# A gelu's square moved from ScalarE to GpSimd, in a kernel that interleaves attention and a dense layer

## The chip, the cores and the metric

The kernel runs on one core of a Trainium2 chip. The metric is device time in microseconds (us). The engines are named as the profile names them: PE (TensorE matmul), PEld (TensorE weight load, which overlaps PE), DVE (VectorE), ACT (ScalarE), POOL (GpSimd) and SP (SyncE, which issues DMAs).

## The reference

An input `x` of 2048 tokens by 512 features goes through two branches, and a gate of each token mixes them.

```python
g = sigmoid((x * gate_w).sum(-1, keepdims=True))
# a: attention, 32 heads of 16, each query sees the 256 latest keys
q, k, v = split_heads(x @ wqkv)
scores = where(mask, q @ k.T * 16 ** -0.5, -1e9)
a = (softmax(scores) @ v) @ wo
# b: dense layer with a tanh gelu, 512 -> 1792 -> 512
b = gelu(x @ w1 + b1, approximate=True) @ w2 + b2
out = g * a + (1 - g) * b
```

The gelu of x1 is 0.5 x1 (1 + tanh(0.79788 (x1 + 0.044715 x1^3))). The kernel forms it as (1 + tanh(GS * x1 * (x1^2 + GC))) * x1, with GC = 1/0.044715 and GS = 0.79788 * 0.044715, and leaves the factor 0.5 to a later step.

## The kernel before, in words

**Precision.** Every dense product is made of three matmuls: each operand is split into a rounded high part and the low remainder, and high*high, high*low and low*high are summed in PSUM (`mm3`, L101 to L103). So every weight and every hidden tile has a split: one copy to the high part, one subtract for the low part. For weights that is ACT (L156) and, for those of the dense layer, POOL (L160).

**Dense work.** The program `dense` first makes q, k, v in four token tiles of 512 (`qkv`), then runs the dense layer in eight turns of `mlp` (two halves of the hidden features, four token tiles each), and last the output projection (`final`). A turn makes seven products `u` [128 features x 512 tokens], each of 12 matmuls into one of two PSUM banks (`d`). Each `u` is given to `gelu`, which makes a tile `h` (high and low part). Then the turn makes four products `y` [128 tokens x 512], each of which takes the seven `h` in order with three matmuls each (21 matmuls into one bank). The weights of the second half are loaded and split in later parts of the run, some of them during the last turn of the first half.

**Attention.** It goes in 128 units (8 groups of four heads by 16 blocks of 128 tokens). In each unit TensorE makes four products `sm` (L389), whose row maxima DVE takes (L394, tile `jm` and `M`), and, six units later, four products `st` (L433), whose exp ACT takes into `pt` (L445). POOL zeroes the corners of `pt` outside the window (L437, L440), and TensorE multiplies `pt` with v (`pv`, L465). Every second unit the row maxima are negated and split on DVE (`nm`, L405 and L406), turned by a matmul (`mp`, L413) and written by ACT as extra rows of `qs` (L418). `sm` has three PSUM banks, `st` two, `pv` one.

**What sets the order.** PE, ACT, DVE and POOL each carry out their instructions in the order in which the program issues them. A small planner sets it: a modelled time `now` goes forward with each matmul issued, and `after(ns, fn)` puts a step into a list that is issued when `now` has reached its due time. `fill` pulls dense matmuls between the attention's matmuls, some 2345 ns of modelled dense work for each unit. `need(key)` issues steps early where a later one depends on them. So the due times are no delays on the chip: they set where a step stands in its engine's queue.

**The gelu.** Each gelu is a chain of seven steps over one 128x512 f32 tile, by their due times after the first:

- x1 = u + b1, on ACT, out of PSUM (L556)
- f1, sq = (u + b1)^2, on ACT, out of PSUM again (L559)
- f2, sq = (sq + GC) * x1, on DVE (L562)
- f3, tanh of sq, on ACT (L565)
- f4, x1 = (sq + 1) * x1, on DVE (L568)
- f5, the high part of h, a copy on DVE (L571)
- f6, the low part of h, a subtract on POOL (L574)

`x1` and `sq` are SBUF tiles with two buffers each. `GELU` (L749) holds the due times of f1 to f6.

Of the kernel before, what the change touches and what calls it, by code (L numbers as in the profile page):

```python
# [12 lines left out]
AF = mybir.ActivationFunctionType  # L13
# [19 lines left out]
def gated_mix(ctx: ExitStack, tc: tile.TileContext, x, wqkv, wo, w1, b1, w2, b2, gate_w, out):  # L33
    nc = tc.nc
# [10 lines left out]
    def f32(ap):  # L45
        return ap.bitcast(F32)
# [23 lines left out]
    b1c = cp.tile([128, NF], F32, name="b1c")  # L70
# [37 lines left out]
    def after(ns, fn, *args):  # L108
        now[1] += 1
        heapq.heappush(todo, (now[0] + ns, now[1], fn, args))  # L110
# [441 lines left out]
    def gelu(p, f, h):  # L552

        x1 = sb.tile([128, T], F32, tag="x1", bufs=2, name=f"x1{h.name}")
        sq = sb.tile([128, T], F32, tag="sq", bufs=2, name=f"sq{h.name}")
        nc.scalar.activation(x1, p, AF.Identity, bias=b1c[:, f:f + 1])  # L556

        def f1():
            nc.scalar.activation(sq, p, AF.Square, bias=b1c[:, f:f + 1])  # L559

        def f2():
            nc.vector.scalar_tensor_tensor(sq, sq, GC, x1, op0=ALU.add, op1=ALU.mult)  # L562

        def f3():
            nc.scalar.activation(sq, sq, AF.Tanh, scale=GS)  # L565

        def f4():
            nc.vector.scalar_tensor_tensor(x1, sq, 1.0, x1, op0=ALU.add, op1=ALU.mult)  # L568

        def f5():  # L570
            nc.vector.tensor_copy(h[:, 0], x1)  # L571

        def f6():
            nc.gpsimd.tensor_sub(h[:, 1], x1, f32(h[:, 0]))  # L574
            done.add(h.name)
        for ns, fn in zip(GELU, (f1, f2, f3, f4, f5, f6)):
            after(ns, fn)
# [168 lines left out]
LEAD = 6  # L746
START = 117e3
NORM = 6000
GELU = (700, 1500, 2300, 3300, 4200, 5000)  # L749
XAT = 3  # L750
ORDER = 'mspf'
XOR = 1
# [26 lines left out]
```

## Time and profile before

| | us |
|---|---|
| median of 3 runs | 812.53 (812.45 to 814.32) |
| the profiled execution | 813.36 |
| its span in the profile | 811.4 |
| PE busy | 788.5 (97%) |
| PEld busy | 616.6 (76%) |
| DVE busy | 513.7 (63%) |
| ACT busy | 483.4 (60%) |
| POOL busy | 338.7 (42%) |

A busy time is the sum of an engine's instructions in the profile. The ends of matmuls are modelled, so a busy PE can hold waits that the weight loads (PEld) show better. The granted TensorE clock is at its full value in every part of the span. The first gelu starts at 153.8 us from the span's start, the last at 727.8.

### The profile page before, as it was taken

Reading aid. Unit: us, or ns where it says so; the run is one execution under the profiler, and the core shown is the slowest. Engines: PE = TensorE matmul, PEld = TensorE weight load, DVE = VectorE, ACT = ScalarE, POOL = GpSimd, SP = SyncE. Lnnn points to the kernel's source line nnn. Section 1 sums busy time; section 2 is a strip of 40 time slices with the busy share of each in tenths; the row PEclk is TensorE's granted clock in tenths of the full one; section 3 lists DMA queues with packets and bytes.
Section 4 is the critical chain, followed back from the end, with each engine's and each line's share of the span. In section 5 each row is a group of like instructions: output and inputs, shape, how many; then the busy total and the mean of one; then the engine's idle time right before and its main releaser. Section 6 shows DMA issues by size and latency. Waiting matters only on the chain.

```text
span 811.4 us, 14841 instructions
## 1 busy us (share of the span) xinstructions
PE 788.5 (97%) x4694; PEld 616.6 (76%) x4694; DVE 513.7 (63%) x1517; ACT 483.4 (60%) x993; POOL 338.7 (42%) x611
## 2 busy tenths in 40 slices
PE   8999999999999999999999999999999999999998
PEld 6788888867877777688767867877777778777767
DVE  5433332887478758856885688568757865784353
ACT  4434423587568557755875677567656764876631
POOL 3200002396336425542784386336524552574100
PEclk9999999999999999999999999999999999999999
DMA  8985856536542734443234555542664363335873
GB/s 260 387 308 195 304 174 211 195 89 215 164 137 66 227 116 119 122 156 104 86 101 132 171 156 173 152 143 86 192 179 129 99 202 113 97 118 186 249 260 117
DMA packets 94925, 135.72 MB, mean 167 GB/s; under 512 B 32256, under 2 KB 43776, under 8 KB 94848
## 3 DMA queue, kind: packets, MB, share of 16 engines
q1 hardware_dynamic: 94848, 134.79, 52.3%
q8 instruction: 37, 0.61, 0.3%
q14 instruction: 40, 0.33, 0.1%
HBM read 79.70 MB, written 55.05 MB: 166 GB/s over the span
## 4 chain that ended last, share of the span: by engine, by line
PE 78%; DVE 8%; ACT 7%; DMA 2%; issue 2%; SPq 1%; POOL 1%; POOLq 0%; DVEq 0%; ACTq 0%
PE st L433 9%; PE pv L465 9%; PE sm L389 8%; PE y L101 6%; PE y L103 6%; PE y L102 6%; PE u L101 4%; PE u L102 4%; PE u L103 4%; PE qk L101 3%; PE qk L103 3%; PE qk L102 3%; DVE jm L394 2%; ACT pt L445 2%; PE v L103 2%
## 5 line engine op out<-in xcount | busy, mean ns | idle before, releaser
L394 DVE CUSTOM_DVE_ANT_0 jm<-sm,mask 128x384 bf16<-128x384 f32 (+2 forms) x512 | 270.6, 528 | 150.1 <-PE sm L389 128.7
L445 ACT ACTIVATE pt<-st 128x384 f32<-128x384 f32 (+2 forms) x512 | 231.0, 471 | 120.6 <-PE st L433 102.9
L437 POOL TENSOR_SCALAR_AFFINE_SELECT pt<-pt 128x256 f32<-128x256 f32 x256 | 122.3, 478 | 248.8 <-ACT pt L445 248.2
L433 PE MATMUL st<-qs,ks 128*128 128x384 f32 (+2 forms) x512 | 172.1, 338 | 8.1 <-ACT pt L445 7.1
L389 PE MATMUL sm<-ks,qs 96*128 96x384 f32 (+2 forms) x512 | 169.6, 332 | 1.8 <-DVE M L394 0.8
L433 PEld LDWEIGHTS st<-qs,ks 128*128 128x128 f32 x512 | 97.0, 190 | 37.1 <-ACT pt L445 19.4
L389 PEld LDWEIGHTS sm<-ks,qs 96*128 96x128 f32 x512 | 96.2, 188 | 26.0 <-DVE M L394 5.2
L440 POOL TENSOR_SCALAR_AFFINE_SELECT pt<-pt 128x256 f32<-128x256 f32 x224 | 101.9, 455 | 0.0
L465 PE MATMUL pv<-pt,vbuf 128*32 128x384 f32 (+2 forms) x1408 | 91.6, 389 | 0.1
L101 PE MATMUL y<-w,h 128*128 128x512 f32 x224 | 89.4, 399 | 0.0
L103 PE MATMUL y<-w,h 128*128 128x512 f32 x224 | 87.7, 391 | 1.3 <-POOL h L574 1.3
L102 PE MATMUL y<-w,h 128*128 128x512 f32 x224 | 87.7, 391 | 0.0
L574 POOL TENSOR_TENSOR h<-x1h,h 128x512 fp32r<-128x512 f32 x56 | 72.5, 1294 | 35.6 <-DVE h L571 35.2
L101 PE MATMUL u<-mx,w 128*128 128x512 f32 x196 | 79.3, 404 | 0.0
L102 PE MATMUL u<-mx,w 128*128 128x512 f32 x196 | 76.7, 391 | 0.0
L103 PE MATMUL u<-mx,w 128*128 128x512 f32 x196 | 76.6, 391 | 0.0
L418 ACT ACTIVATE qs<-mp,odd 16x256 fp32r<-16x256 f32 x128 | 53.0, 460 | 38.9 <-PE mp L413 37.9
L465 PEld LDWEIGHTS pv<-pt,vbuf 128*32 128x32 f32 x1408 | 38.5, 109 | 37.2 <-issue 24.2
L562 DVE SCALAR_TENSOR_TENSOR sqh<-sqh,x1h 128x512 f32<-128x512 f32 x56 | 51.6, 921 | 13.2 <-ACT sqh L559 13.2
L565 ACT ACTIVATE sqh<-sqh 128x512 f32<-128x512 f32 x56 | 35.5, 634 | 36.8 <-DVE sqh L562 36.2
L160 POOL TENSOR_TENSOR w<-raw_w,w 128x512 fp32r<-128x512 f32 x28 | 38.4, 1370 | 40.3 <-ACT w L156 40.2
L256 DVE TENSOR_TENSOR qke<-qk,qke 128x512 fp32r<-128x512 f32 x32 | 22.1, 691 | 51.3 <-ACT qke L253 49.6
(122 smaller groups left out, 1247.7 us busy)
## 6 DMA issues: line engine op xcount, KB each, us to landing
mx<-XT SPq DMA_DIRECT2D x24, 512.0 KB
SQ<-qke SPq DMA_DIRECT2D x16, 512.0 KB
SK<-qke SPq DMA_DIRECT2D x16, 512.0 KB
qs<-SQ SPq DMA_DIRECT2D x64, 128.0 KB
ND<-nd SPq DMA_DIRECT2D x32, 256.0 KB
ks<-SK SPq DMA_DIRECT2D x60, 128.0 KB
raw_w<-in_B_w_dram SPq DMA_DIRECT2D x28, 256.0 KB
SV<-vx SPq DMA_DIRECT2D x16, 272.0 KB
```

The costliest lines, as they stand in the source:

```text
L101: nc.tensor.matmul(p, lh, rh, start=first, stop=False)
L102: nc.tensor.matmul(p, lh, rl, start=False, stop=False)
L103: nc.tensor.matmul(p, ll, rh, start=False, stop=last)
L389: nc.tensor.matmul(p[:, :w], qs[0:96, pr, b * 128:(b + 1) * 128], ks[0:96, pr, s, k0:k0 + w], start=True, stop=True)
L394: nc.vector.tensor_tensor_reduce(junk[:, :w], p[:, :w], mask[:, 384 - w:384], 1.0, -3e38, ALU.add, ALU.max, M[:, b % RB, i:i + 1])
L418: nc.scalar.activation(qs[96:112, :, cols], p[96:112].unsqueeze(1).broadcast_to([16, 2, 128]), AF.Copy, scale=odd[96:112, b:b + 1])
L433: nc.tensor.matmul(p[:, :w], ks[:, pr, s, kb * 128:(kb + 1) * 128], qs[:, pr, kb * 128:kb * 128 + w], start=True, stop=True)
L437: nc.gpsimd.affine_select(out=pt[:, :, 0:128], in_=pt[:, :, 0:128], pattern=[[0, 2], [1, 128]], compare_op=ALU.is_ge, fill=0.0, base=0, ch ...
L440: nc.gpsimd.affine_select(out=pt[:, :, 256:384], in_=pt[:, :, 256:384], pattern=[[0, 2], [-1, 128]], compare_op=ALU.is_ge, fill=0.0, base= ...
L445: nc.scalar.activation(pt[:, s, :w], p[:, :w], AF.Exp, scale=SCALE)
L465: nc.tensor.matmul(pv[32 * i:32 * i + 32, q - c * T:e - c * T], vt[:, 68 * (kb % NB) + 17 * i:68 * (kb % NB) + 17 * i + 32], pts[g_, kb, i ...
L574: nc.gpsimd.tensor_sub(h[:, 1], x1, f32(h[:, 0]))
```

## The change

The square is formed on POOL, as x1 times x1 out of SBUF, and no longer on ACT out of PSUM. The due times of f2 to f6 move 700 ns later; that of f1 stays.

```diff
         nc.scalar.activation(x1, p, AF.Identity, bias=b1c[:, f:f + 1])
 
         def f1():
-            nc.scalar.activation(sq, p, AF.Square, bias=b1c[:, f:f + 1])
+            nc.gpsimd.tensor_mul(sq, x1, x1)
 
         def f2():
             nc.vector.scalar_tensor_tensor(sq, sq, GC, x1, op0=ALU.add, op1=ALU.mult)
...
-GELU = (700, 1500, 2300, 3300, 4200, 5000)
+GELU = (700, 2200, 3000, 4000, 4900, 5700)
```

## The prediction

> **What bounds the kernel now.** I read the page first, for the engines and the chain that ended last; then stretches of time, to find where TensorE loses anything; then what TensorE's weight loads waited for; then the groups by line; last, single instructions in order of time.
>
> ```profile
> PE 788.5 (97%) x4694; PEld 616.6 (76%) x4694; DVE 513.7 (63%) x1517; ACT 483.4 (60%) x993; POOL 338.7 (42%) x611
> ...
> PE 78%; DVE 8%; ACT 7%; DMA 2%; issue 2%; SPq 1%; POOL 1%; POOLq 0%; DVEq 0%; ACTq 0%
> ```
>
> TensorE is the bound by share, but a fifth of the chain runs over other engines. To see where, I cut the attention part into stretches of eight attention units (32 score matmuls each). Eight stretches hold the `u` products and so the gelus (first table: four of them and the sum of all eight); seven hold only `y` products between the same attention work (second table: the last and the sum). The columns are us, then the busy time of PE, PEld, DVE, ACT and POOL with counts.
>
> ```profile
> 157.10:197.30 40.20, 37.94 (x217) 28.71 (x216) 35.35 (x93) 31.38 (x65) 34.11 (x44) 1.00 0.43 132
> ...
> 383.70:423.30 39.60, 38.19 (x233) 29.04 (x233) 33.59 (x95) 33.26 (x69) 29.78 (x43) 1.00 0.36 104
> 460.80:502.40 41.60, 39.11 (x233) 28.86 (x232) 35.69 (x97) 33.41 (x70) 30.97 (x43) 1.00 0.49 145
> ...
> sum 316.60, PE 304.47 PEld 230.24 DVE 265.75 ACT 249.06 POOL 210.36; mean PE 38.06 PEld 28.78 DVE 33.22 ACT 31.13 POOL 26.30
> ```
>
> ```profile
> 652.70:689.10 36.40, 36.40 (x249) 28.97 (x248) 21.62 (x81) 19.50 (x45) 13.49 (x31) 1.00 0.50 158
> sum 254.40, PE 253.05 PEld 201.08 DVE 148.87 ACT 135.14 POOL 91.51; mean PE 36.15 PEld 28.73 DVE 21.27 ACT 19.31 POOL 13.07
> ```
>
> A `y` stretch takes 254.40/7 = 36.34 us, with TensorE never idle in the row shown. A `u` stretch takes 316.60/8 = 39.58. So the gelu stretches lose 316.60 - 8 x 36.34 = **25.9 us** in all, and nothing is lost elsewhere that this change touches. In them DVE is 84% busy, ACT 79%, POOL 66%: no engine is full, so the loss is in-order queues making TensorE wait. Who did it, over the whole of these stretches:
>
> ```profile
> PEld st L433 <- ACT pt L445: 19.2, 38, 1.4
> PEld mp L413 <- issue: 11.1, 28, 0.6
> PEld mp L413 <- DVE M L394: 6.6, 16, 0.6
> PEld mp L413 <- DVE nm L406: 5.4, 8, 1.5
> PEld sm L389 <- DVE M L394: 5.2, 13, 0.9
> PEld sm L389 <- ACT qs L418: 2.7, 5, 0.9
> PEld mp L413 <- DVE sqh L562: 2.1, 4, 0.6
> PEld y L103 <- POOL h L574: 1.8, 1, 1.8
> PEld pv L465 <- POOL pt L440: 1.3, 6, 0.2
> ```
>
> "Issue" names nobody and I leave it out. ACT: 19.2 + 2.7 = 21.9. DVE: 6.6 + 5.4 + 5.2 + 2.1 = 19.3. POOL: 1.8 + 1.3 = 3.1. These are idle times of the weight loads, which overlap with matmuls; together 44.3 against 25.9 us really lost, a factor 0.58. So ACT costs 12.8 us of time, DVE 11.2, POOL 1.8. Work that each engine does in the `u` stretches beyond the `y` ones: ACT 249.06 - 8 x 19.31 = 94.6, DVE 265.75 - 8 x 21.27 = 95.6, POOL 210.36 - 8 x 13.07 = 105.8. That gives an average price of one us of added work: **ACT 0.135, DVE 0.117, POOL 0.017** us. It is an estimate of mine; near a full queue the next us costs more than the average one. I use it as a scale.
>
> **The change, part by part.**
>
> **ACT loses the second pass (a gain).**
>
> ```profile
> L559 ACT ACTIVATE sqh<-u,b1c 128x512 f32<-128x512 f32 x56 | 38.5, 687 | 0.0
> ```
>
> 56 x 687 ns = 38.5 us. At the average price that is 38.5 x 0.135 = 5.2 us. Does it sit in the way of the exps that TensorE waits for? In 17 of the 30 longest waits of a score matmul for an exp this pass ran just ahead of the exps (in the last of them with one weight split between). First and last of the 17:
>
> ```profile
> 183.48 0.68 ACT L559 ACTIVATE sqh<-u,b1c 128x512 f32<-128x512 f32 x1
> ...
> 184.59 0.19 PEld L433 LDWEIGHTS st<-qs,ks 128*128 128x128 f32 x1 [0.75 <-ACT pt L445]
> ...
> 717.98 0.19 PEld L433 LDWEIGHTS st<-qs,ks 128*128 128x128 f32 x1 [0.71 <-ACT pt L445]
> ```
>
> 17 x 0.687 x 0.58 = 6.8 us. In the others the tanh held ACT while it waited for DVE, and that stays. Ends: 0 (the next wait takes over) and -12.8 (all of ACT's share); I take **-6**, between 5.2 and 6.8. The PSUM bank of `u` is read once and free 0.69 us sooner; no row shows TensorE waiting for it, so 0.
>
> **POOL gains 56 products.** Nothing shows this exact form; the nearest row is the subtract with two f32 operands of the same size.
>
> ```profile
> L574 POOL TENSOR_TENSOR h<-x1h,h 128x512 fp32r<-128x512 f32 x56 | 72.5, 1294 | 35.6 <-DVE h L571 35.2 <-DVE nm L405 0.4
> L160 POOL TENSOR_TENSOR w<-raw_w,w 128x512 fp32r<-128x512 f32 x28 | 38.4, 1370 | 40.3 <-ACT w L156 40.2
> ```
>
> 56 x 1.294 = 72.5 us, nearly all in the `u` stretches: 210.4 + 72.5 = 282.8 of 316.6, or 89%, fuller than DVE is now. In the first stretch, where POOL also splits weights, 34.11 + 6 x 1.294 = 41.9 us of work stand against 40.2 us of time. POOL takes its queue in order: behind a late square stand the selects of `pt` (then pv on TensorE), the weight splits and the previous gelu's subtract. Ahead of it may stand a subtract or a split, 1.3 us. And the first DVE step, L562, now waits for POOL: with POOL free, 0.687 + 1.294 = 1.98 us after x1 starts, where two ACT passes took 2 x 0.687 = 1.37; its slot moves by 0.7, so that alone costs nothing, but any POOL delay is passed on. Behind L562 on DVE stand the row maxima that free TensorE's `sm` banks, the `nm` that the next `mp` needs, and the tanh on ACT with the exps behind it. Price: low, POOL's average now, 72.5 x 0.017 = 1.2 us; high, the price that ACT and DVE show at 79 and 84% busy, 72.5 x 0.135 = 9.8. At 89% it is nearer to the high end: **+6**.
>
> **Two engines in each other's way.**
>
> ```profile
> L562 DVE SCALAR_TENSOR_TENSOR sqh<-sqh,x1h 128x512 f32<-128x512 f32 x56 | 51.6, 921 | 13.2 <-ACT sqh L559 13.2
> L568 DVE SCALAR_TENSOR_TENSOR x1h<-sqh,x1h 128x512 f32<-128x512 f32 x56 | 42.8, 764 | 7.5 <-ACT sqh L565 7.5
> ...
> L406 DVE SCALAR_TENSOR_TENSOR nm<-M,nm 128x8 fp32r<-128x8 f32 x64 | 17.7, 277 | 2.2
> ```
>
> ```profile
> L562 DVE SCALAR_TENSOR_TENSOR sqh<-sqh,x1h x56: 677/775/1775, 155.1 to 730.6; 128x512 f32<-128x512 f32 x56
> ...
> L568 DVE SCALAR_TENSOR_TENSOR x1h<-sqh,x1h x56: 682/689/1739, 156.9 to 732.4; 128x512 f32<-128x512 f32 x56
> ...
> L406 DVE SCALAR_TENSOR_TENSOR nm<-M,nm x64: 167/171/1279, 142.4 to 738.2; 128x8 fp32r<-128x8 f32 x64
> ```
>
> ```profile
> 401.02 1.28 POOL L160 TENSOR_TENSOR w<-raw_w,w 128x512 fp32r<-128x512 f32 x1
> ...
> 401.50 1.35 DVE L562 SCALAR_TENSOR_TENSOR sqh<-sqh,x1h 128x512 f32<-128x512 f32 x1
> ```
>
> The second fence has minimum, median and maximum of one instruction. L562 takes 677 ns alone, and 1.35 us here, beside a POOL subtract. Stretching now: 56 x 0.244 = 13.7, 56 x 0.082 = 4.6, 64 x 0.110 = 7.0 us: 25.3 us, over 84 POOL subtracts 0.30 us each. A square cannot meet its own gelu's DVE steps, only its neighbour's, so between 0 and 56 x 0.30 = 16.9 us of DVE; half, 8.4, at 0.117 to twice that is 1.0 to 2.0: **+1.5**; ends 0 and 16.9 x 0.234 = 4.0.
>
> The Trainium skill, page "SBUF — State Buffer", section "SBUF: two separate sides", says that VectorE and GpSimd share one pair of ports as an exclusive lock, and that the one who comes second waits until the other's instruction is over. The row agrees: 402.30 plus 0.68 would end at 402.98, and L562 ended at 402.85.
>
> **The five later steps move by 700 ns.** Each of the eight turns makes seven `h` tiles, and `y` takes them in order; the seventh's subtract was late once and barely in time another time:
>
> ```profile
> 426.49 0.50 PE L103 MATMUL y<-w,h 128*128 128x512 f32 x1 [1.35 <-POOL h L574]
> ```
>
> ```profile
> 733.59 1.29 POOL L574 TENSOR_TENSOR h<-x1h,h 128x512 fp32r<-128x512 f32 x1 [2.07 <-DVE h L571]
> ```
>
> ```profile
> 735.34 0.39 PE L103 MATMUL y<-w,h 128*128 128x512 f32 x1
> ```
>
> The one turn already waited, so all of the 0.7 is lost; the last turn has 735.34 - (733.59 + 1.29) = 0.46 of slack and loses 0.24: 0.9 us at least. With one more POOL product ahead (1.29): 1.99 + 1.53 = 3.5. I take **+2**. The `x1` buffers, held 0.7 longer, I cost at nothing: two of them cover the next gelu's 5.65 us (316.6/56) twice.
>
> **Sum:** -6 + 6 + 1.5 + 2 = **+3.5 us**. The profiled execution took 813.36 us (811.4 of span, 1.96 around it), so 816.9 of its own; it lies 0.83 above the median of the three runs, 812.53, on which I put the forecast: **816.0**.
>
> **Rivals.**
>
> *The relief of ACT wins.* POOL stands idle before the selects for long (it waits for exps), so the square could start as x1 ends and L562 find it done. Then -6.8 + 1.2 (POOL at its average) + 0.5 + 0.9 = -4.2: 808.3. It decides where L562's idle before it stays at its 13.2 us or under; against it stands POOL's 66% in these very stretches. Chance 0.30.
>
> *Both sides cancel*: the exps come sooner, DVE's steps as much later, 812.5. Chance 0.18.
>
> *POOL becomes the bound where weights are split* (the three stretches shown). With squares these hold 41.9, 29.78 + 9.06 = 38.8 and 30.97 + 9.06 = 40.0 us of work; if POOL is idle for a tenth besides (DVE at its fullest, 35.35 of 40.20, for an eighth), they need 46.5, 43.1 and 44.5 in place of 40.2, 39.6 and 41.6: +12.7, and with the other terms (-6 + 1.5 + 2) +10.2: 822.7. For it speaks that the work already fits into none of the first stretch's 40.2 us, against it that a `y` stretch follows with POOL a third busy. Chance 0.12.
>
> *Every DVE step that meets a square waits it out.* L568, the copy and about one `nm` step come in each 5.65 us; 3.1 x 1.294/5.65 = 0.71 meetings of 0.65 us, 26 us of DVE, at twice the price 6.1 us in place of 1.5: 820.6. Chance 0.07. That is the skill's rule on the shared ports taken in full.
>
> **How the numbers follow.** About 0.3% (2.4 us) is what can be told from no change. The forecast, slower by some us, gets 0.33 and by itself covers 813.5 to 821. Slower: 0.33 + 0.12 + 0.07 = 0.52; same 0.18; faster 0.30. Range: below, ACT's gain toward -9 with the rest near its low ends (0.9 + 0.5 + 2) gives -5.6; above, no gain with 9.8 + 4.0 would be +14: 807 to 826.
>
> **What would show it.** L559's group gone from ACT, a POOL group of 56 at about 1.3 us in its place. ACT's waits of `st` from 19.2 to about 10. L562's idle now ended by POOL, above 20 us; L562's mean at or above 921 ns. `y` waiting for `h` in more than one turn. `u` stretches at 320 us in sum, `y` stretches unchanged. Wrong if L562 hardly waits for POOL, or if TensorE's waits for `mp` and `sm` do not grow.

## The result, and the profile after

The changed kernel took **853.9 us** (median of 5 runs, 852.57 to 856.44) against 812.53 for the kernel before: ratio 1.0507, 95% interval 1.0484 to 1.0530. It is slower by 41 us, where I had forecast 3.5 and a range up to 826. One execution among the experiments (of the square due sooner) took 1272.79 us at a granted clock of 0.557, where all others had 0.98 or more; it is in no median here.

The page of the changed kernel, its first lines and the engines on the chain that ended last:

```profile
span 850.9 us, 14785 instructions
...
PE 799.7 (94%) x4694; PEld 619.7 (73%) x4694; DVE 535.3 (63%) x1517; ACT 453.1 (53%) x937; POOL 401.7 (47%) x667
...
PE 64%; DVE 13%; POOL 8%; ACT 6%; issue 5%; DMA 2%; SPq 0%; POOLq 0%; DVEq 0%
```

ACT lost 30 us, POOL gained 63. (A busy time of the page counts the overlap of two records once, so ACT's fell by less than the 38.5 us of the pass.) No engine but TensorE is over two thirds busy, and yet the chain now runs over DVE and POOL for a fifth of the span (9% before). The stretches of eight attention units again, cut at the same units: first the sum of the eight with `u` products, then of the seven with `y` products alone.

```profile
sum 352.50, PE 313.10 PEld 233.57 DVE 282.83 ACT 220.72 POOL 264.38; mean PE 39.14 PEld 29.20 DVE 35.35 ACT 27.59 POOL 33.05
```

```profile
sum 257.20, PE 254.46 PEld 200.59 DVE 153.07 ACT 134.78 POOL 96.59; mean PE 36.35 PEld 28.66 DVE 21.87 ACT 19.25 POOL 13.80
```

The `u` stretches grew from 316.6 to 352.5 us, +35.9 of the 39.5 us by which the span grew; the `y` stretches grew by 2.8, mostly at their starts, where `y` waits for the last `h`. What TensorE's weight loads waited for from the first to the last of these stretches:

```profile
PEld st L433 <- ACT pt L445: 41.7, 43, 3.1
PEld pv L465 <- issue: 22.6, 108, 0.3
PEld mp L413 <- DVE nm L406: 11.7, 12, 2.3
PEld mp L413 <- issue: 10.2, 25, 0.6
PEld sm L389 <- DVE M L394: 8.7, 14, 1.3
PEld mp L413 <- DVE M L394: 7.0, 16, 0.6
PEld sm L389 <- ACT qs L418: 4.0, 5, 1.7
PEld y L103 <- POOL h L574: 2.8, 3, 1.6
```

The wait for the exps is no shorter for an ACT with less to do: it doubled, 19.2 to 41.7. Why, the page's groups say (busy and mean of one, then the idle time before it and who ended it):

```profile
L565 ACT ACTIVATE sqh<-sqh 128x512 f32<-128x512 f32 x56 | 35.3, 631 | 101.9 <-DVE sqh L562 101.9
...
L562 DVE SCALAR_TENSOR_TENSOR sqh<-sqh,x1h 128x512 f32<-128x512 f32 x56 | 61.6, 1101 | 31.4 <-POOL sqh L559 31.1
...
L559 POOL TENSOR_TENSOR sqh<-x1h 128x512 f32<-128x512 f32 x56 | 60.4, 1078 | 8.7 <-ACT x1h L556 8.7
```

The tanh (L565) holds ACT idle for 101.9 us while it waits for L562; in the kernel before it was 36.2:

```profile
L565 ACT ACTIVATE sqh<-sqh 128x512 f32<-128x512 f32 x56 | 35.5, 634 | 36.8 <-DVE sqh L562 36.2
```

L562 waits 31 us for POOL's square and then takes 1101 ns in the mean. Minimum, median and maximum of the square and of L562:

```profile
L559 POOL TENSOR_TENSOR sqh<-x1h x56: 1032/1042/1474, 153.5 to 766.7; 128x512 f32<-128x512 f32 x56
...
L562 DVE SCALAR_TENSOR_TENSOR sqh<-sqh,x1h x56: 681/872/1767, 154.9 to 768.2; 128x512 f32<-128x512 f32 x56
```

Half of the L562 take over 872 ns, where the shortest take 681. Does POOL hold them? As L562 started, a POOL instruction was already running, with 100 ns or more to go, in 49 of the 56 cases (30 in the kernel before). For 35 of them DVE had stood idle; in 33 of these 35 POOL's next instruction had begun 66 to 88 ns before L562 (21 selects, seven weight splits, five subtracts), and these 33 took 1195 ns in the mean, the other two 693. One case in order of time:

```profile
510.86 1.05 POOL L559 TENSOR_TENSOR sqh<-x1h 128x512 f32<-128x512 f32 x1
...
511.86 1.27 POOL L160 TENSOR_TENSOR w<-raw_w,w 128x512 fp32r<-128x512 f32 x1
511.94 1.74 DVE L562 SCALAR_TENSOR_TENSOR sqh<-sqh,x1h 128x512 f32<-128x512 f32 x1 [1.23 <-POOL sqh L559]
...
513.72 0.63 ACT L565 ACTIVATE sqh<-sqh 128x512 f32<-128x512 f32 x1 [2.98 <-DVE sqh L562]
...
514.25 0.85 ACT L445 ACTIVATE pt<-st 128x384 f32<-128x384 f32 x2
...
514.78 0.45 PE L433 MATMUL st<-qs,ks 128*128 128x384 f32 x1 [2.68 <-ACT pt L445]
```

These lines show the mechanism. The square ends at 511.9. POOL goes straight on to its next instruction, a weight split, at 511.86. L562 gets the word 80 ns later, and is held until the split is over, 513.13, plus about its own length. The tanh has stood at the head of ACT's queue for 2.98 us, two exps behind it; TensorE stands for 2.68 us.

Such stands have a second price. In the windows below (us, then PE, PEld, DVE, ACT, POOL busy, then the granted clock as a share) TensorE is mostly idle for 3.3 us and then is granted half its clock for 3.4:

```profile
425.00:428.30 3.30, 1.20 (x6) 1.08 (x7) 3.16 (x9) 2.00 (x4) 3.12 (x5) 1.00 0.63 180
428.30:431.70 3.40, 3.40 (x11) 2.81 (x10) 1.30 (x5) 2.08 (x4) 3.40 (x5) 0.50 0.46 128
```

The kernel before shows no such drop while the attention runs; the changed one shows three (at 428, 500 and 742 us), at most 3 x 1.7 = 5 us. The Trainium skill, page "TensorE: Matmul & The Clock Gate", section "What's actually happening", says that the clock goes to a half after an idle window of about 3.4 us and comes back after a busy one; length and share agree with these rows. The window ahead of the drop was not wholly idle here: TensorE was busy for 1.20 of its 3.30 us.

### The profile page after: what moved, and what is told of

Same layout as the page of the kernel before. It is cut to its first block, busy times and chain, and to the rows that moved or that the text cites. A ratio compares the mean times of both kernels' runs of the same rounds, so it can differ in the third digit from the quotient of the medians.

```text
span 850.9 us, 14785 instructions
## 1 busy us (share of the span) xinstructions
PE 799.7 (94%) x4694; PEld 619.7 (73%) x4694; DVE 535.3 (63%) x1517; ACT 453.1 (53%) x937; POOL 401.7 (47%) x667
## 4 chain that ended last, share of the span: by engine, by line
PE 64%; DVE 13%; POOL 8%; ACT 6%; issue 5%; DMA 2%; SPq 0%; POOLq 0%; DVEq 0%
PE st L433 7%; PE pv L465 7%; PE sm L389 6%; PE y L103 5%; PE y L101 5%; PE y L102 5%; DVE sqh L562 4%; DVE jm L394 4%; PE qk L103 3%; PE qk L101 3%; PE qk L102 3%; POOL sqh L559 3%; PE u L101 3%; ACT pt L445 3%; PE u L102 2%
## 5 line engine op out<-in xcount | busy, mean ns | idle before, releaser
L437 POOL TENSOR_SCALAR_AFFINE_SELECT pt<-pt 128x256 f32<-128x256 f32 x256 | 124.2, 485 | 237.0 <-ACT pt L445 236.4
L433 PE MATMUL st<-qs,ks 128*128 128x384 f32 (+2 forms) x512 | 174.0, 342 | 28.4 <-ACT pt L445 27.2
L440 POOL TENSOR_SCALAR_AFFINE_SELECT pt<-pt 128x256 f32<-128x256 f32 x224 | 106.6, 476 | 0.0
L565 ACT ACTIVATE sqh<-sqh 128x512 f32<-128x512 f32 x56 | 35.3, 631 | 101.9 <-DVE sqh L562 101.9
L562 DVE SCALAR_TENSOR_TENSOR sqh<-sqh,x1h 128x512 f32<-128x512 f32 x56 | 61.6, 1101 | 31.4 <-POOL sqh L559 31.1
L101 PE MATMUL u<-mx,w 128*128 128x512 f32 x196 | 80.5, 411 | 0.0
L102 PE MATMUL u<-mx,w 128*128 128x512 f32 x196 | 77.7, 397 | 0.0
L103 PE MATMUL u<-mx,w 128*128 128x512 f32 x196 | 77.6, 396 | 0.0
L465 PEld LDWEIGHTS pv<-pt,vbuf 128*32 128x32 f32 x1408 | 38.9, 110 | 38.3 <-issue 24.1
L559 POOL TENSOR_TENSOR sqh<-x1h 128x512 f32<-128x512 f32 x56 | 60.4, 1078 | 8.7 <-ACT x1h L556 8.7
```

The costliest lines, as they stand in the source:

```text
L101: nc.tensor.matmul(p, lh, rh, start=first, stop=False)
L102: nc.tensor.matmul(p, lh, rl, start=False, stop=False)
L103: nc.tensor.matmul(p, ll, rh, start=False, stop=last)
L433: nc.tensor.matmul(p[:, :w], ks[:, pr, s, kb * 128:(kb + 1) * 128], qs[:, pr, kb * 128:kb * 128 + w], start=True, stop=True)
L437: nc.gpsimd.affine_select(out=pt[:, :, 0:128], in_=pt[:, :, 0:128], pattern=[[0, 2], [1, 128]], compare_op=ALU.is_ge, fill=0.0, base=0, ch ...
L440: nc.gpsimd.affine_select(out=pt[:, :, 256:384], in_=pt[:, :, 256:384], pattern=[[0, 2], [-1, 128]], compare_op=ALU.is_ge, fill=0.0, base= ...
```

## The experiments

Three theories stood at first. A: a chain (POOL's square late, L562 late, tanh late, exps late). B: POOL's added load by itself, through its queue and its meetings with DVE. C: the later due times. The kernels were timed beside the kernel before; differences below are to its median in the same runs. Where two experiments are compared with each other, or one with the change, the medians come from different runs, in which the kernel before lay between 812.5 and 813.6, so such a difference is good to about 1 us.

**The due times alone (C).**

```diff
-GELU = (700, 1500, 2300, 3300, 4200, 5000)
+GELU = (700, 2200, 3000, 4000, 4900, 5700)
```

> The square stays on ACT as before; only the due times of f2 to f6 move 700 ns later, as in the change. Theory A (the 41 us come from a chain: L562 waits for POOL's square, the tanh waits for L562, the exps stand behind the tanh) expects little here, 811 to 817: the last h of a turn arrives up to 0.7 us later, but L562 finds its square done. Theory C (the later due times themselves cost it, through late h tiles and x1 buffers held longer) expects 830 or more.

817.11 us, +3.8 (ratio 1.0045, 1.0030 to 1.0060). C falls. L562's group in this run is the base for what follows: it hardly waits.

```profile
L562 DVE SCALAR_TENSOR_TENSOR sqh<-sqh,x1h 128x512 f32<-128x512 f32 x56 | 55.3, 987 | 1.4 <-ACT sqh L559 1.3
```

**ACT's relief alone.**

```diff
-            nc.scalar.activation(sq, p, AF.Square, bias=b1c[:, f:f + 1])
+            pass
...
-            nc.vector.scalar_tensor_tensor(sq, sq, GC, x1, op0=ALU.add, op1=ALU.mult)
+            nc.vector.scalar_tensor_tensor(sq, x1, GC, x1, op0=ALU.add, op1=ALU.mult)
```

> Leaves the square out: L562 reads x1 in its place, so the second ACT pass is gone and POOL gets nothing; due times of before. It shows what the relief of ACT is worth by itself. My prediction priced it at -6 us (806 to 808); if the relief is worth nothing, 811 to 814; if the ACT pass was worth all of ACT's share, 800.

808.53 us, -4.8 (0.9932, 0.9911 to 0.9954). The gain that I priced at -6 is real, and it comes where I put it, from 19.4 us in the kernel before:

```profile
PEld st L433 <- ACT pt L445: 11.8, 27, 1.0
```

The run also spares L562 the wait for a square (DVE's idle time before it falls from 13.2 to 1.8 us), so not all of the 4.8 need be ACT's.

**POOL's product beside, waited for by nobody at first sight.**

```diff
             nc.scalar.activation(sq, p, AF.Square, bias=b1c[:, f:f + 1])
+            nc.gpsimd.tensor_mul(h[:, 1], x1, x1)
```

> The square stays on ACT and due times are those of before, but POOL also forms x1 times x1, into the low half of h, which its own later subtract overwrites: nobody waits for it. So POOL's load and its meetings with DVE's two-operand steps are those of the change, without the chain. Theory A expects a part of the loss only, 815 to 828. Theory B (POOL's load and the shared access to SBUF by themselves) expects nearly all of it, 840 or more.

838.29 us, +25 (1.0325, 1.0296 to 1.0353): between the two. It was not as free of waits as I meant: L568 (one line lower here) overwrites x1 and has to wait until POOL has read it.

```profile
DVE x1h L569 <- POOL h L560: 8.6, 6, 2.2
```

**The same with the later due times.** The two edits above (product beside, GELU of the change) together:

> ACT keeps the square that is used; POOL forms x1 times x1 too, into the low half of h (only the later step that overwrites x1 has to wait for POOL to have read it); the later due times of the change. Against the changed kernel it lacks the wait of L562 for POOL and keeps the ACT pass. If POOL's load is the cause (theory B), 842 to 850: the 25 us of the product beside plus the 4 us of the shift plus a bit. If the wait of L562 for the square (theory A) carries the rest, 825 to 838, since at these due times L562 falls behind the product and meets it less.

831.14 us, +17.5 (1.0211, 1.0174 to 1.0247). Against the shift alone POOL's product costs 831.14 - 817.11 = **14.0** us, and 23 us of the 41 are not in it. Here L568 waits for POOL 1.5 us only.

**POOL as busy, but reading nothing.**

```diff
             nc.scalar.activation(sq, p, AF.Square, bias=b1c[:, f:f + 1])
+            nc.gpsimd.memset(f32(h[:, 1]), 0.0)
+            nc.gpsimd.memset(f32(h[:, 1]), 0.0)
```

> As the run before it, but in place of the product POOL does two memsets of the same half of h, about 1.05 us together, which read nothing and depend on nothing. So POOL's queue is as full, while nothing of it holds up a DVE step that reads two operands. If POOL's loss is its queue (late selects, late subtracts), the time is that of the product beside, within 4 us; if it is the meeting with DVE at the shared access to SBUF, it is that of the shift alone, 815 to 822.

823.04 us, +9.5 (1.0107, 1.0079 to 1.0135). POOL is nearly as full, 30.5 + 29.3 us against 65.0 of the product:

```profile
L561 POOL MEMSET h<- 128x512 f32 x56 | 30.5, 545 | 3.2
L560 POOL MEMSET h<- 128x512 f32 x56 | 29.3, 524 | 0.0
```

The time lies between the two expectations, nearer to the shift alone. So of the 14.0 us, 823.04 - 817.11 = 5.9 are the fuller queue, and 8.1 come with a product that reads SBUF and x1: L562 took 896 ns in the mean beside the memsets and 1037 beside the product.

**The wait for POOL's queue, without the load.**

```diff
             nc.scalar.activation(sq, p, AF.Square, bias=b1c[:, f:f + 1])
+            nc.gpsimd.tensor_mul(sq[:, 0:1], x1[:, 0:1], x1[:, 0:1])
```

> The chain without the load: the ACT square stays, the later due times of the change, and POOL rewrites one column of the square (128x1, some 0.1 us), so L562 still has to wait until POOL's queue comes to that place, but POOL gains almost no work. Theory A, in its strong form (the wait for POOL's queue is the cause), expects 830 or more; if only POOL's work counts, the 817 of the shift alone, to 820.

821.76 us, +8.2 (1.0105, 1.0060 to 1.0150): 4.7 over the shift alone. The strong form of A falls too: the hand-over to POOL is cheap as long as POOL's queue is short. But L562 takes as long as in the change, 1102 ns in the mean, now that a POOL instruction releases it:

```profile
L563 DVE SCALAR_TENSOR_TENSOR sqh<-sqh,x1h 128x512 f32<-128x512 f32 x56 | 61.7, 1102 | 9.7 <-POOL sqh L560 9.3
```

So a long L562 is not dear by itself: here it costs 4.7 us together with the wait.

**The change, its L562 reading PSUM.**

```diff
-            nc.vector.scalar_tensor_tensor(sq, sq, GC, x1, op0=ALU.add, op1=ALU.mult)
+            nc.vector.scalar_tensor_tensor(sq, sq, GC, p, op0=ALU.add, op1=ALU.mult)
```

> The change, but L562 multiplies by u in PSUM in place of x1 in SBUF (this leaves b1 out of one factor): it still waits for POOL's square, but reads only one operand from SBUF. In the changed kernel POOL's next instruction starts as the square ends, and 43 of the 56 L562 take over 800 ns. If that hold-up is the missing part, L562 goes back to one length near 0.7 us, the tanh's wait falls from 102 to about 75 us, and the time to 840 to 848. If the wait for the square alone is the cause, 852 or more; PSUM's bank is held some 3 us longer, which could add a little.

833.36 us, against 853.9: **20.5 us back** from the operand of one instruction (1.0232, 1.0190 to 1.0275, over the kernel before). Better than I expected. It still waits for POOL as long, 33.3 us, but it is never held:

```profile
L562 DVE SCALAR_TENSOR_TENSOR sqh<-sqh,u 128x512 f32<-128x512 f32 x56 | 38.3, 685 | 33.3 <-POOL sqh L559 33.1
...
L562 DVE SCALAR_TENSOR_TENSOR sqh<-sqh,u x56: 675/686/690, 155.5 to 745.6; 128x512 f32<-128x512 f32 x56
```

POOL's busy time falls as well, from 401.7 to 383.2 us, so POOL, too, is held less in this run; the run does not part the two. It has one drop of the clock where the change has three, which is at most 3.4 of the 20.5 us.

**Other due times for the change.** f2 to f6 later by 1400 ns more:

```diff
-GELU = (700, 2200, 3000, 4000, 4900, 5700)
+GELU = (700, 3600, 4400, 5400, 6300, 7100)
```

> The change with f2 to f6 due another 1400 ns later (3600, 4400, 5400, 6300, 7100). Theory A expects L562 to wait for POOL seldom (under 8 us in all, 31 in the changed kernel) and the tanh's wait for L562 to fall from 102 us to about 40; exps on time again; but each turn's last h comes 1.4 us later still, up to 10 us over eight turns: 825 to 840. Theory B expects no better than 850.

840.27 us, 14 better than the change. L562's wait for POOL fell to 4.3 us and the tanh's to 59, and `y` pays for it: it waits for `h` seven times, 7.4 us in all.

```profile
PEld st L433 <- ACT pt L445: 23.7, 39, 2.3
...
PEld y L103 <- POOL h L574: 7.4, 7, 1.7
```

And the square due sooner, `GELU = (100, 2200, 3000, 4000, 4900, 5700)`:

> The change with the square due 100 ns after x1 in place of 700: it stands further ahead in POOL's queue, before selects and splits that came up in between. Theory A expects the square to start about 0.3 us sooner (now 1.47 us after x1 starts on average) and 3 to 12 us back: 842 to 851. If the wait for the square is no cause, 854, or more, since the selects wait for x1 behind it.

845.8 us (median of its other three executions), 8 better. L562's wait for POOL is down to 13.9 us, the tanh's to 85.6. Both runs follow the chain, and neither comes near the kernel before.

**The subtract on DVE, the square on POOL.** `nc.gpsimd.tensor_sub` of f6 becomes `nc.vector.tensor_sub`:

> The change with the last subtract (L574) on DVE in place of POOL: POOL's work is then close to that of before (56 squares for 56 subtracts), its queue ahead of the square is shorter, and DVE has 56 x 0.69 = 38 us more. If POOL's doubled load is the root, the square starts about 1.0 us after x1 and the time falls to 820 to 835, DVE's work included. If the place of the square in the chain is the root whatever POOL's load, 845 or more.

834.56 us (1.0248, 1.0202 to 1.0295): 19 back with POOL's load that of before (339.0 us busy against 338.7). So nearly half of the loss goes with POOL's load; in the half that stays, DVE has 56 subtracts more.

**The square on DVE.** `nc.gpsimd.tensor_mul` becomes `nc.vector.tensor_mul`, with the due times of before:

> The square on DVE, as x1 times x1, with the due times of before: ACT is relieved as in the change, the square needs no hand-over to L562, POOL gets nothing, DVE 56 x 0.69 = 38 us more. By my price of DVE's work (0.117 to 0.234 us each) 4.5 to 9 us more, less the 5 us of ACT's relief: 812 to 818. If DVE is the engine that all the losses run through, 825 or more.

850.0 us (1.0444, 1.0401 to 1.0488). I was off by over 30 us. The first reading is that DVE now waits for x1 at the head of its queue:

```profile
DVE sqh L559 <- ACT x1h L556: 23.2, 26, 2.4
```

So the square was moved behind x1, `GELU = (1400, 2200, 3000, 4000, 4900, 5700)`:

> The square on DVE as in the run with 850 us, but due 1400 ns after x1 in place of 700, and f2 to f6 as in the change. If the square's waiting for x1 at the head of DVE's queue (23 us) caused that loss, 818 to 828: 4 of shift, -5 of ACT's relief, 5 to 9 of DVE's work and some of the tanh's wait. If DVE's work is the cause, 845 or more.

849.44 us. That wait is gone (3.0 us) and the time is not: the cost is DVE's own time. Its busy time is 562.9 us, 40.8 more than with the shift alone; 38 of that are 56 squares of 679 ns, the shortest, and the mean square took 1049.

```profile
L559 DVE TENSOR_TENSOR sqh<-x1h 128x512 f32<-128x512 f32 x56 | 58.8, 1049 | 3.3 <-ACT x1h L556 3.0
L562 DVE SCALAR_TENSOR_TENSOR sqh<-sqh,x1h 128x512 f32<-128x512 f32 x56 | 51.2, 915 | 0.4
```

**Versions of the kernel before that hold DVE less.** Its subtract on DVE:

> The kernel before with its last subtract on DVE in place of POOL, square on ACT, due times of before. It takes the 56 products of POOL away that meet DVE's two-operand steps, for 38 us of DVE. If those meetings cost DVE as much as it gains in work, 808 to 816; if DVE's plain work counts, 818 to 825.

814.76 us: 1.0021, 1.0001 to 1.0041, no difference worth the name. Then x1 in place in PSUM, so that neither L562 nor L568 can be held:

```diff
-        nc.scalar.activation(x1, p, AF.Identity, bias=b1c[:, f:f + 1])
+        nc.scalar.activation(p, p, AF.Identity, bias=b1c[:, f:f + 1])
...
-            nc.scalar.activation(sq, p, AF.Square, bias=b1c[:, f:f + 1])
+            nc.scalar.activation(sq, p, AF.Square)
...
-            nc.vector.scalar_tensor_tensor(sq, sq, GC, x1, op0=ALU.add, op1=ALU.mult)
+            nc.vector.scalar_tensor_tensor(sq, sq, GC, p, op0=ALU.add, op1=ALU.mult)
...
-            nc.vector.scalar_tensor_tensor(x1, sq, 1.0, x1, op0=ALU.add, op1=ALU.mult)
+            nc.vector.scalar_tensor_tensor(x1, sq, 1.0, p, op0=ALU.add, op1=ALU.mult)
```

> The kernel before, but ACT forms x1 in place in PSUM, and L562 and L568 read it there, so neither reads two operands from SBUF (square on ACT, due times of before). If their hold-up beside POOL's subtracts and selects costs time in the kernel before too, they go to about 0.69 us each (921 and 764 now) and the time falls by 2 to 6 us, to 807 to 811; if it is hidden there, no change. The PSUM bank of u is held some 4 us longer, to the fourth step; if TensorE needs it sooner, it loses up to 10 us.

814.3 us (1.0017, 1.0004 to 1.0030). The tanh's wait for DVE fell from 36 to 13 us and that for the exps from 19 to 12, and a new wait took their place, for PSUM's bank:

```profile
PEld u L101 <- DVE x1h L568: 12.7, 18, 1.3
PEld st L433 <- ACT pt L445: 12.3, 24, 1.0
```

The same with earlier due times, `(100, 900, 1700, 2500, 3600, 4400)` and `(400, 1200, 2000, 2900, 3900, 4700)`:

> x1 in place in PSUM as in the run before it, square on ACT, with due times 600 to 800 ns earlier (100, 900, 1700, 2500, 3600, 4400). If the wait for the bank of u eats the gain, that wait falls from 12.7 us to under 6 and the time to 807 to 811. If steps that are due earlier only wait longer at the head of DVE's and ACT's queues, 814 or more.

> The same with half of the shift (400, 1200, 2000, 2900, 3900, 4700): bank waits of about 8 us and 809 to 813 by the first view; 814 or more by the second.

812.4 us (0.9990, 0.9971 to 1.0008) and 812.21 us (0.9984, 0.9967 to 1.0000). The bank's wait falls from 12.7 to 1.0 and 2.3 us, and the wait for the exps is back at 22 in both (here the second):

```profile
PEld st L433 <- ACT pt L445: 21.9, 46, 1.1
```

No version that still forms the square beats the kernel before by more than its measurement can tell.

## Why the prediction was wrong

**The account that the runs give.** Shift +3.8; relief of ACT -4.8; POOL's product beside +14.0 (5.9 queue, 8.1 with its reading); the wait of L562 for POOL's queue +4.7; L562 held while POOL is as full as in the change +20.5. Sum 38.2, of 41.4. This is no partition, and that it nearly closes is in part luck. The terms come from different runs and share something: L562 is as long in the run with one column. And the 20.5 are the worth of freeing L562 of all its hold-up, 61.6 - 38.3 = 23.3 us; 51.6 - 38.3 = 13.3 of those it had in the kernel before, where freeing L562 and L568 gained at most 0.2% (814.3, 812.4 and 812.21 us, with PSUM's bank held longer). What is shown is that the operand of L562 decides about half of the loss as long as POOL has the work of the change.

**What held.** The direction. ACT's relief: -6 told, -4.8 measured. The shift: +2 told, +3.8. Signs told in advance: L562's idle ended by POOL and over 20 us (31.1), its mean over 921 ns (1101), `y` late in more than one turn. Two signs failed: the wait of `st` for the exps was to fall to about 10 us and was 41.7, and the `u` stretches were to take 320 us and took 352.5.

**The step that failed: the price of a held DVE and POOL**, in the terms "POOL gains 56 products" (+6) and "two engines in each other's way" (+1.5). I divided TensorE's waits by each engine's extra work and got 0.117 us of time for one us of DVE, 0.017 to 0.135 for POOL, and took the last as the top of what POOL could cost: 9.8 us, of which I took 6. That is an average over work most of which delayed nobody. The runs give the price at the margin. Take as held the idle before the two-operand step and its busy time, against the run with the shift alone (1.4 + 55.3):

- one column: 9.7 + 61.7, so 14.7 us more held, for 4.7 us of time: 0.3
- the square on DVE behind x1: 58.8 + 3.3 + 51.2 + 0.4, so 57 us more, for 849.4 - 817.1 + 4.8 = 37, of which five drops of the clock can be up to 8.5: 0.65 at most
- the change against itself with L562 reading PSUM: 31.4 + 61.6 against 33.3 + 38.3, so 21.4 us, for 20.5: about 1

So one us of DVE's time ahead of the tanh cost three to eight times my price of 0.117, in stretches where DVE was already 84% busy. That price belongs to the place in the chain and not to DVE's work as such: with the subtract at the end of the chain moved to DVE (the run with 814.76) DVE's busy time grew from 513.7 to 532.7 us and the time by 1.7. That run takes 56 subtracts off POOL as well. My own figure of 84% should have warned me, as should the tanh: I named that it stands behind L562 with the exps behind it, and then priced it by the average.

**A second step failed in its reason.** For the two engines in each other's way I wrote that a square meets only its neighbour's steps, took half of the meetings, 8.4 us of DVE (16.9 at most), and priced them at 1.5. But L562 is released by the *end* of a POOL instruction, and at that moment POOL's *next* one starts. Where POOL has something waiting, that one is first and L562 is held: not by chance but by construction, in 33 of 35 waits. DVE's busy time grew by 21.6 us with no instruction more (1517 in both), 10.0 of it in L562. So the amount was over twice what I took; at my highest price, 0.234, it would still have been 5 us, and the price is the larger error.

**The rivals.** That every step which meets a square waits it out named the right resource and priced it at 6.1 us with the same false price. That both sides cancel (812.5) fell with the wait for the exps, which doubled. POOL full in the stretches with weight splits (822.7) holds in part: POOL did not become full, 264.4 of 352.5 us in the `u` stretches, 75%, and stretches without splits lost too. The relief of ACT winning would have needed L562's idle to stay at 13 us; it was 31.

**A term that I mis-sized the other way**: a POOL product took 1078 ns, not 1294. And the upper end of my range, 9.8 + 4.0, left out the +2 of the later due times, while the lower end counted them.

The Trainium skill, page "SBUF — State Buffer", section "SBUF: two separate sides", which I cited for a single row, describes the hold-up: whoever of the two starts first has the shared ports for the whole instruction. The lines from 510.86 on agree with it, and so does L562 at 675 to 690 ns once its second operand is in PSUM.

## What to carry to other kernels

Price a move by the queue that waits, not by the busy time that it shifts: when an in-order chain (POOL, then DVE, then ACT, with TensorE's operands behind ACT) gets a slower link, each us of delay can cost up to a full us, as here, even where every engine but TensorE is idle for a fifth of the time. Before letting GpSimd release a VectorE step with two SBUF operands, ask what GpSimd does next: where it had work waiting, it had started by then, and the VectorE step waited for it; an operand in PSUM took it out of the way. A relief of 38 us on an engine that is not the bound was worth 5.

## What the runs showed of the hardware that I had not expected

A POOL product of one tensor with itself takes 1042 ns (median, 128x512 f32) and a subtract of two tensors 1286; with the product's output as fp32r it is 1042 as well:

```profile
L560 POOL TENSOR_TENSOR h<-x1h x56: 1032/1042/1502, 153.9 to 745.6; 128x512 fp32r<-128x512 f32 x56
```

Whether that lies in the operand read twice or in product against subtract was not tried. And a stand of TensorE can cost up to 1.7 us more through the halved clock that follows, which I had in no term. The three drops came behind stands of 2.12, 1.91 and 1.87 us, while no drop came behind the two longest, 2.68 and 2.42 us: the length of one stand does not settle it.
